# The output projection of a fused attention and gated FFN kernel, in pairs of token tiles with seven products of quarters

## The chip, the cores and the metric

The kernel runs on one core of one Trainium2 chip. The metric is the device time of one launch in microseconds (us); lower is better. A core has five engines that run side by side, each in its own program order, and wait for one another by semaphores: TensorE (PE, matrix products into PSUM; PEld is its weight load), VectorE (DVE), ScalarE (ACT), GpSimd (POOL) and SyncE (SP, which issues DMAs).

## The reference

Four batches, eight heads, 768 tokens, head size 64. Queries and keys are each assigned to the nearest of 16 centroids of their head; a query attends only to keys of its own cluster. The result, as 3072 tokens by 512, goes through a gated FFN:

```python
q_assign = argmax(q_n @ c_n.T); k_assign = argmax(k_n @ c_n.T)      # per head
scores = where(q_assign[:, None] == k_assign[None, :], q @ k.T / sqrt(64), -1e9)
x = softmax(scores) @ v                                             # -> [3072, 512]
gate = 1 / (1 + exp(-(x @ w_gate)))                                 # [512, 1536]
out = (gate * (x @ w_val)) @ w_out                                  # w_out [1536, 512] -> [3072, 512]
```

## The kernel before

**Attention.** The work goes batch by batch and head by head in *steps*. A step multiplies one chunk of 128 keys with half a batch's queries (384): one matmul `sc` of 384 columns (L655), an Exp on ACT into `es` (L660), and, one to three steps later, three matmuls `av` (L678) that add up the values, with a column of ones for the softmax's sum. After a head's last step DVE and POOL normalise (`t`, `rec`, `xp`, L342 to L360), and a transpose puts the result into `xT`. The heads of a later batch are prepared alongside: casts and differences (`hl`, L1217 and L1218), transposes by DMA into `T`, logits against the centroids (`lg`), their sum and maximum on DVE (`lgs` L421, `mx` L432), one-hot rows (`oh` L434, L441), and sums over the values (L302, L308, L309, L318).

**FFN.** `ffn_atoms` makes the work of a block of 384 tokens (half a batch, so eight blocks; t0 is 0 or 384). For each of 12 chunks `fc` of the 1536 hidden columns there is a `gate` (four matmuls of 384 columns, L480, then Tanh on ACT, L488) and a `val` (four matmuls, L500, then DVE's `hT[fc] = (th + 1) * v`, L507, in fp16). Sigmoid is 0.5 (1 + tanh(x/2)); the factor 0.5 is put in when the output leaves PSUM. Then for each of the block's three token tiles `outp` adds up 12 matmuls of 512 columns in one PSUM bank `o` (L520), with `hT` as the stationary operand, `wo` as the moving one; the bank is emptied to `ob` by ACT (L529) or DVE (L527) and stored. The last tile of all is done by `closing` in parts of 256, 128 and 128 columns (`o_end`, L552).

**Order.** Everything is emitted in one order written out by hand; each engine keeps the order in which its instructions are emitted. Attention steps come one after another, preparations at a step named in `SCHED` (`at`, `plan`), and the FFN pieces wait in `queue`. After each step's scores `ffn_run(ns)` takes pieces off the queue for about `ns` nanoseconds of PE time (`ns02`, `ns10` and so on, by batch and quarter), so PE alternates between attention and FFN. The last batch's first block is queued shortly before its attention ends and the last block after it, so most of both runs with no attention beside it.

**PSUM.** Eight banks: a `ring` of four (scores, gates, values, logits), two for `av`, and two (`op`, used in turn) for `o` and, through `turns`, for some transposes and logits.

Of the kernel before, what the change touches and what calls it, by code (L numbers as in the profile page):

```python
# [98 lines left out]
def kernel(  # L99
# [43 lines left out]
    hl2p = pool("hl2", 2)  # L143
    tp = pool("T", 10)
    tbp = pool("TB", 4)
# [9 lines left out]
    osp = pool("os", 3)  # L155
    smp = pool("sm", 3)
# [6 lines left out]

    def turns(n=768, dt=HP, name="turns"):
        return op.tile([128, n], dt, tag="o", name=name)
# [17 lines left out]
    def raw(side):  # L183
        return rawp.tile([128, 2, NCH, 64], FP, tag=f"{side}raw", name=f"{side}raw", bufs=SCHED.get(f"{side}rb", 4))
# [8 lines left out]
    def load(eng, side, b, p):  # L193
        t = RAW[side, b, p] = raw(side)
        eng.dma_start(out=t, in_=view(side, b, p))
# [6 lines left out]
    def load_chunks(eng, side, p, part):  # L202
        if part == 0:
            RAW[side, 0, p] = raw(side)
        c = slice(Q0, NCH) if part else slice(0, Q0)
        eng.dma_start(out=RAW[side, 0, p][:, :, c], in_=view(side, 0, p)[:, :, c])

    def load_half(eng, side, part):
        if (side, 0, 0) not in RAW:
            RAW[side, 0, 0] = raw(side)  # L210
        c = slice(0, Q0) if side == "q" else slice(KC, NCH) if part else slice(0, KC)
        eng.dma_start(out=RAW[side, 0, 0][:, 0, c], in_=view(side, 0, 0)[:, 0, c])
# [36 lines left out]

    c2 = const.tile([128, 2, D], FP, name="c2")  # L250
# [33 lines left out]
    vas = [const.tile([128, 2, NCH, 65], HP, name=f"va{i}") for i in range(6)]  # L284
    for t in vas:
        DVE.memset(t[:, :, :, 64:65], 1.0)
    for t in vss:
        DVE.memset(t[:, :, 64:65], float(NCH))
# [177 lines left out]

    def ffn_atoms(xT, t0, n, b, ch, final=False):
        hT = htp.tile([128, NFC, 384], HP, name="hT")
        gv, outs = [], []
        OA = SCHED.get(f"oa{b}{t0}", SCHED.get("oa", 4))  # L470
        cost = NDC * max(n, 80) / 2.4 + 3

        def gate(fc, st, part):
            def f():
                need(("w", fc // WQ, 0), *(("x", b, p, t0 // 128 + c) for p in range(NP) for c in range(n // 128)))
                if part == 0:
                    st.append(bank(512, name="g"))
                g = st[0]
                for dc in range(GA * part, GA * part + GA):
                    PE.matmul(  # L480
                        out=g[:, 0:n], lhsT=wg[fc // WQ][:, dc, fc % WQ, :],
                        rhs=xT[:, dc, t0 : t0 + n],
                        start=(dc == 0), stop=(dc == NDC - 1),
                    )
                if part < NDC // GA - 1:
                    return
# [6 lines left out]
        def val(fc, st, part):  # L493
            def f():
                need(("w", fc // WQ, 1))
                if part == 0:
                    st.append(bank(512, name="v"))
                w = st[2]
                for dc in range(GA * part, GA * part + GA):
                    PE.matmul(  # L500
                        out=w[:, 0:n], lhsT=wv[fc // WQ][:, dc, fc % WQ, :],
                        rhs=xT[:, dc, t0 : t0 + n],
                        start=(dc == 0), stop=(dc == NDC - 1),
                    )
                if part < NDC // GA - 1:
                    return
                DVE.scalar_tensor_tensor(  # L507
                    hT[:, fc, 0:n], st[1][:, 0:n], 1.0, w[:, 0:n], ALU.add, ALU.mult
                )

            return f

        def outp(t, part, st):
            def f():
                if part == 0:
                    need(*(("wo", i) for i in range(WOP)))
                    st.append(op.tile([128, DM], FP, tag="o", name="o"))
                o = st[0]
                for fc in range(OA * part, OA * part + OA):
                    PE.matmul(  # L520
                        out=o, lhsT=hT[:, fc, bass.ts(t, 128)], rhs=wo[fc // WON][:, fc % WON, :],
                        start=(fc == 0), stop=(fc == NFC - 1),
                    )
                if part == NFC // OA - 1:
                    ob = osp.tile([128, DM], FP, name="ob")
                    if t % 2 or SCHED.get(f"ob{b}{t0}", 0):
                        DVE.tensor_scalar(ob, o, 0.5, None, ALU.mult)  # L527
                    else:
                        ACT.activation(ob, o, AF.Copy, scale=0.5)  # L529

                    def store(ob=ob):
                        SP.dma_start(
                            out=out[b * S : (b + 1) * S].rearrange("(p c) m -> p c m", c=NCH)[
                                :, ch[t], :
                            ],
                            in_=ob,
                        )

                    d_ = SCHED.get("sd", 0)
                    if d_ > 0 and b < B - 2:  # L540
                        at(step_no[0] + d_, store)
                    else:
                        store()

            return f

        def closing(t, a, z):
            def f():
                w = z - a
                o = bank(w, name="o_end")  # L550
                for fc in range(NFC):
                    PE.matmul(  # L552
                        out=o, lhsT=hT[:, fc, bass.ts(t, 128)],
                        rhs=wo[fc // WON][:, fc % WON, a:z],
                        start=(fc == 0), stop=(fc == NFC - 1),
                    )
                ob = osp.tile([128, w], FP, tag="ob_end", name="ob_end")
                if a:
                    DVE.tensor_scalar(ob, o, 0.5, None, ALU.mult)
                else:  # L560
                    ACT.activation(ob, o, AF.Copy, scale=0.5)
                SP.dma_start(
                    out=out[b * S : (b + 1) * S].rearrange("(p c) m -> p c m", c=NCH)[
                        :, ch[t], a:z
                    ],
                    in_=ob,
                )

            return f

        for fc in range(NFC):
            st = []
            for i in range(NDC // GA):
                gv.append((cost * GA / NDC, gate(fc, st, i)))
            for i in range(NDC // GA):
                gv.append((cost * GA / NDC, val(fc, st, i)))
        for t in range(n // 128):
            st = []
            if final and t == n // 128 - 1:
                outs.append([(900, closing(t, a, z)) for a, z in SCHED.get("cl", [(0, 256), (256, 384), (384, 512)])])  # L580
            else:
                outs.append([(OA * 216, outp(t, i, st)) for i in range(NFC // OA)])
        return gv, outs

    queue = []
    GA = SCHED.get("ga", 4)

    def ffn_block(*a):
        gv, outs = ffn_atoms(*a)
        for x in gv:  # L590
            queue.append(x)
        for o in outs:
            queue.extend(o)

    def ffn_two(a, b_):
        gv, outs = ffn_atoms(*a)
        gv2, outs2 = ffn_atoms(*b_)
        seq = gv + gv2[0:2]
        for i, o in enumerate(outs):
            seq += o + gv2[2 + 2 * i : 4 + 2 * i]  # L600
        seq += gv2[2 + 2 * len(outs) :]
        for o in outs2:
            seq += o
        queue.extend(seq)
# [112 lines left out]
    def plan(name, step, f):  # L717
        at(SCHED.get(name, step), f)
# [361 lines left out]
    for x in SCHED.get("lo", ["v0", "k1", "q1", "v1", "k2", "q2", "v2", "k3", "q3", "v3"]):  # L1080
        if x == "v0" and SCHED.get("v0h", 0):
            RAW["v", 0, 0] = raw("v")
# [124 lines left out]
    for i in range(WOP):  # L1207
        plan(f"wo{i}", 44 + 6 * i, lambda i=i: load_wo(i))

# [142 lines left out]
```

## Time and profile before

| | |
|---|---|
| three runs | 326.07, 326.52, 327.12 us, median 326.52 |
| the profiled execution | span 326.4 us from the first to the last instruction; the page gives no other time of it |
| busy shares | PE 97%, weight loads 63%, DVE 57%, ACT 72%, POOL 33% |
| granted TensorE clock | 1.00 in every stretch |
| `o` products | 276 of 512 columns, and 36 narrow ones of the last tile |
| `ob` evacuations | 15 on ACT (596 ns each), 8 on DVE (692 ns each), 3 small ones at the end |
| HBM | 106 GB/s over the span |

How to read the lines: a group's row names the line, engine and operation, out<-in by the program's names, the shape (partitions x elements), the count, then the busy time in us and the mean ns of one, then the engine's idle time just before them and who ended it. A row of a stretch gives the stretch, then the busy us and count of PE, PEld, DVE, ACT, POOL, the granted clock, the DMA share and GB/s. A row of the timeline gives start, length, engine, line, operation, and the idle time before. A PE record is longer than its share of the stream, since matmuls overlap: the pace is read from start to start, as the chain of work does. (The chain gives a product's time from where it takes the array over, so its starts lie up to 0.2 us behind those of the records.)

### The profile page before, as it was taken

The numbers are of one execution on the slowest core, as the hardware profiler recorded it, in microseconds if no ns is written. First come the engines' busy times: TensorE is split into PE (matmuls) and PEld (weight loads), VectorE is DVE, ScalarE is ACT, GpSimd is POOL, SyncE is SP. The second block draws the span as 40 slices with busy tenths as digits, with TensorE's granted clock in tenths as the row PEclk, the third lists the DMA queues.
The fourth block names the chain that finished last, engine by engine and source line by source line (L and its number), as shares of the span: only waits on it lengthen the run. The fifth ranks groups of instructions, "written<-read, shape, count | busy, mean of one in ns | idle before, by whom it ended". The sixth has DMA issues, their size and how long they took to land.

```text
span 326.4 us, 8811 instructions
## 1 busy us (share of the span) xinstructions
PE 318.0 (97%) x3366; PEld 205.8 (63%) x3366; DVE 187.4 (57%) x509; ACT 235.6 (72%) x526; POOL 108.4 (33%) x145
## 2 busy tenths in 40 slices
PE   7899999999999989999999999999999999999996
PEld 4788666766666656666566655666566655654654
DVE  6899567766767766657546655666544322441431
ACT  6788988788899878877677777887778877332420
POOL 6887554054345353324222343323200111000000
PEclk9999999999999999999999999999999999999999
DMA  7999995848977797964795574932731012102002
GB/s 209 358 259 179 263 177 91 207 104 206 242 138 197 138 205 162 257 190 85 124 255 110 169 101 130 238 70 50 141 90 38 2 24 78 44 2 94 6 0 96
DMA packets 77994, 45.14 MB, mean 138 GB/s; under 512 B 56896, under 2 KB 75008, under 8 KB 77952
## 3 DMA queue, kind: packets, MB, share of 16 engines
q1 hardware_dynamic: 73984, 39.73, 50.7%
q0 software_dynamic: 3680, 4.72, 8.7%
q8 instruction: 26, 0.43, 0.5%
q14 instruction: 16, 0.13, 0.1%
q10 hardware_dynamic: 288, 0.13, 0.1%
HBM read 28.34 MB, written 6.29 MB: 106 GB/s over the span
## 4 chain that ended last, share of the span: by engine, by line
PE 86%; DMA 4%; POOL 3%; DVE 3%; issue 2%; SPq 1%; ACT 0%; POOLq 0%
PE g L480 19%; PE v L500 19%; PE o L520 17%; PE sc L655 16%; PE av L678 9%; DMA T<-hl 2%; PE lg L406 2%; DMA kraw<-in_k_dram 2%; PE o_end L552 1%; POOL xp L360 1%; POOL hl L883 1%; POOL hl L1004 1%; PE t_ps L904 0%; PE lg L393 0%; PE t_ps L787 0%
## 5 line engine op out<-in xcount | busy, mean ns | idle before, releaser
L660 ACT ACTIVATE es<-sc 128x384 f16<-128x384 f32 x384 | 175.6, 492 | 42.6 <-PE sc L655 35.6
L655 PE MATMUL sc<-T 128*128 128x384 f16 x384 | 118.0, 325 | 0.7 <-DVE T L985 0.4
L678 PEld LDWEIGHTS <-es 128*128 128x128 f16 x1152 | 81.6, 98 | 49.1 <-ACT es L660 0.2
L678 PE MATMUL av<-va,es 128*128 128x65 f16 x1152 | 97.6, 194 | 0.0
L507 DVE SCALAR_TENSOR_TENSOR hT<-th,v 128x384 f16<-128x384 f32 x96 | 53.1, 554 | 70.3 <-PE av L678 47.4
L500 PE MATMUL v<-xTb,wv 128*128 128x384 f16 x384 | 78.1, 326 | 0.0
L480 PE MATMUL g<-xTb,wg 128*128 128x384 f16 x384 | 78.0, 326 | 0.0
L520 PE MATMUL o<-wo,hT 128*128 128x512 f16 x276 | 75.1, 379 | 0.0
L488 ACT ACTIVATE th<-g 128x384 f32<-128x384 f32 x96 | 47.2, 491 | 25.7 <-DVE hT L507 17.9
L347 POOL TENSOR_TENSOR xp<-t,rec 128x384 f16<-128x384 f32 (+1 forms) x30 | 21.2, 705 | 107.8 <-DVE rec L344 56.4
L480 PEld LDWEIGHTS <-wg 128*128 128x128 f16 x384 | 37.2, 97 | 20.4
L500 PEld LDWEIGHTS <-wv 128*128 128x128 f16 x384 | 37.4, 98 | 19.9
L655 PEld LDWEIGHTS <-T 128*128 128x128 f16 x384 | 37.1, 97 | 1.2 <-DVE T L985 0.7
L520 PEld LDWEIGHTS <-hT 128*128 128x128 f16 x276 | 26.7, 97 | 16.2
L1218 POOL TENSOR_TENSOR hl<-kraw,hl 128x384 f16<-128x384 f32 x22 | 20.4, 925 | 37.5 <-DVE hl L1217 18.2
L342 DVE TENSOR_TENSOR t<-av,sv 128x390 f32<-128x390 f32 (+1 forms) x30 | 14.4, 480 | 20.5 <-PE av L678 16.2
L1218 POOL TENSOR_TENSOR hl<-qraw,hl 128x384 f16<-128x384 f32 x22 | 21.4, 973 | 10.6 <-DVE hl L1217 10.6
L421 DVE TENSOR_REDUCE lgs<-lg 128x192 f32<-128x384 f32 x23 | 12.7, 554 | 13.6 <-PE lg L406 13.6
L529 ACT ACTIVATE ob<-o 128x512 f32<-128x512 f32 x15 | 8.9, 596 | 10.7 <-PE o L520 10.5
L294 POOL CAST va<-vraw 128x768 f16<-128x768 f32 x16 | 13.7, 857 | 2.1 <-DMA vraw<-in_v_dram 2.1
L527 DVE TENSOR_SCALAR ob<-o 128x512 f32<-128x512 f32 x8 | 5.5, 692 | 13.4 <-PE o L520 13.4
L406 PE MATMUL lg<-cm,T 128*128 128x32 f16 x288 | 11.1, 176 | 1.3 <-DMA T<-hl 1.3
(118 smaller groups left out, 239.2 us busy)
## 6 DMA issues: line engine op xcount, KB each, us to landing
vraw<-in_v_dram SPq DMA_DIRECT2D x16, 384.0 KB, 5.9
out_dram<-ob SPq DMA_DIRECT2D x23, 256.0 KB, 2.3
kraw<-in_k_dram SPq DMA_DIRECT2D x15, 384.0 KB, 4.1
qraw<-in_q_dram SPq DMA_DIRECT2D x12, 384.0 KB, 5.0
wg<-in_moe_w_gate_dram POOLq DMA_DIRECT2D x2, 768.0 KB, 9.5
wv<-in_moe_w_val_dram POOLq DMA_DIRECT2D x2, 768.0 KB, 10.5
wo<-in_moe_w_out_dram POOLq DMA_DIRECT2D x2, 768.0 KB, 8.8
qraw<-in_q_dram SPq DMA_DIRECT2D x7, 192.0 KB, 6.9
```

The costliest lines, as they stand in the source:

```text
L342: DVE.tensor_tensor(t[:, 0:nq, :], av, sv, ALU.add)
L347: (eng or POOL).tensor_tensor(x, t[:, 0:nq, 0:64], bcast(rec[:, 0:nq], 64), ALU.mult)
L406: PE.matmul(out=lg[:, bass.ts(i, 32)], lhsT=t[:, c, :], rhs=cm[:, h].rearrange("p s n -> p (s n)"), start=True, stop=True,)
L480: PE.matmul(out=g[:, 0:n], lhsT=wg[fc // WQ][:, dc, fc % WQ, :], rhs=xT[:, dc, t0 : t0 + n], start=(dc == 0), stop=(dc == NDC - 1),)
L488: ACT.activation(th[:, 0:n], g[:, 0:n], AF.Tanh, scale=0.5)
L500: PE.matmul(out=w[:, 0:n], lhsT=wv[fc // WQ][:, dc, fc % WQ, :], rhs=xT[:, dc, t0 : t0 + n], start=(dc == 0), stop=(dc == NDC - 1),)
L507: DVE.scalar_tensor_tensor(hT[:, fc, 0:n], st[1][:, 0:n], 1.0, w[:, 0:n], ALU.add, ALU.mult)
L520: PE.matmul(out=o, lhsT=hT[:, fc, bass.ts(t, 128)], rhs=wo[fc // WON][:, fc % WON, :], start=(fc == 0), stop=(fc == NFC - 1),)
L655: PE.matmul(out=sc.rearrange("p (c t) -> p c t", t=128), lhsT=s["k"], rhs=s["q"], start=True, stop=True,)
L660: ACT.activation(es, sc, AF.Exp, scale=SCALE)
L678: PE.matmul(out=av[:, a0 + s["c0"] + i, :], lhsT=s["es"][:, bass.ts(i, 128)], rhs=VA[b, p][:, e, s["j"], :], start=(first and i == 0 and a ...
L1218: POOL.tensor_tensor(hl[:, :, 64:128], r, hl[:, :, 0:64], ALU.subtract)
```

## The change

Tokens are taken in pairs of tiles A1 (t1) and A2 (t2), hidden columns in halves f = 0, 1 (six chunks each), output columns in halves of 256. B11, B12, B21, B22 are the quarters of `w_out`. In place of eight products of quarters there are seven (Strassen's scheme in Winograd's form):

- once, four mixed weights (`mix_wo`, each in two parts of 128x768, while the gates of the first block run): T1 = B12 - B11 and T2 = B22 - T1 on DVE, T3 = B22 - B12 and T4 = B21 - T2 on POOL. They lie in `held`, the raw tiles of the first batch's last head pair, which are of no more use then, and T4 in B12's place.
- per pair, four sums on DVE in fp16 (`pair_sums`, 128x768 each): s1 = A2[0] + A2[1], s2 = s1 - A1[0], s4 = A1[1] - s2, s3 = A1[0] - A2[0]. The first two come right after the block's last `hT`, or, for the second pair of a block, after the first pair's p15; the other two after P1.
- per pair, seven products of six matmuls of 256 columns (`pair_out`), by turns in two banks x and y, each continued or restarted as listed, with what reads the bank afterwards:

| product | bank | operands | then |
|---|---|---|---|
| P1 | x, new | A1[0] B11 | ACT copies p1 |
| P4 | y, new | A2[1] T4 | DVE p14 = y + p1 |
| P2 | x, added to P1 | A1[1] B21 | ACT copies to ob of t1, left half |
| P6 | y, added to P4 | s2 T2 | DVE p16 = y + p1 |
| P5 | x, new | s1 T1 | DVE p15 = x + p1 |
| P7 | y, added to P6 | s3 T3 | DVE ob of t2 = y + p14, and y + p15 |
| P3 | x, added to P5 | s4 B22 | DVE ob of t1, right half = x + p16 |

Where the table says "new" the bank is overwritten, else the product adds to what lies there.

Pairs are (0, 1) for the first block of a batch and (2, 3), (4, 5) for the second, so there are twelve, and the first block's third tile is done with the second block. The next pair's P1 takes the bank that the last P3 did not use. While a pair is under way, `turns` takes its bank from the ring. The factor 0.5 moves: the ones column becomes 2, which halves x, so Tanh needs no scale and the output no factor. To make room, `T` has 8 buffers for 10, `va` 5 for 6, raw inputs 3 for 4. The `ns` of the quarters are some 3.5% smaller (all but `ns10`), and `lag01` is 8 for 4.5.

```diff
-    tp = pool("T", 10)
-    tbp = pool("TB", 4)
+    tp = pool("T", 8)
...
+    def mix_wo(i, c, eng):
+        done.add(("wt", i, c))
+        o, a, z, f = [
+            (T1, B12, B11, ALU.subtract), (T3, B22, B12, ALU.subtract),
+            (T2, B22, T1, ALU.subtract), (T4, B21, T2, ALU.subtract),
+        ][i]
+        c = slice(3 * c, 3 * c + 3)
+        eng.tensor_tensor(o[:, c], a[:, c], z[:, c], f)
...
-                ACT.activation(th[:, 0:n], g[:, 0:n], AF.Tanh, scale=0.5)
+                ACT.activation(th[:, 0:n], g[:, 0:n], AF.Tanh)
...
+                if fc == NFC - 1:
+                    sums[0]["one"]()
...
+        def one():
+            add(1, tok(b, t2, 0), tok(b, t2, 1), ALU.add)
+            add(2, st[1], tok(b, t1, 0), ALU.subtract)
+
+        def two():
+            add(4, tok(b, t1, 1), st[2], ALU.subtract)
+            add(3, tok(b, t1, 0), tok(b, t2, 0), ALU.subtract)
...
+        def end1():
+            copy(acc("p1"), st["x"])
+            sm["two"]()
+
+        def end4():
+            plus(acc("p14"), st["y"], st["p1"])
...
+        def end5():
+            plus(acc("p15"), st["x"], st["p1"])
+            if after:
+                after()
+
+        def end7():
+            plus(st["ob", 1][:, lo_], st["y"], st["p14"])
+            plus(st["ob", 1][:, hi_], st["y"], st["p15"])
+            store(1, t2)
+
+        def end3():
+            plus(st["ob", 0][:, hi_], st["x"], st["p16"])
...
+        steps = [
+            ("x", A(t1, 0), B11, True, end1), ("y", A(t2, 1), T4, True, end4),
+            ("x", A(t1, 1), B21, False, end2f), ("y", M(2), T2, True, end6),
+            ("x", M(1), T1, True, end5), ("y", M(3), T3, False, end7),
+            ("x", M(4), B22, False, end3),
+        ]
...
+                for c in range(g, g + G):
+                    PE.matmul(
+                        out=st[z], lhsT=a[:, c, :], rhs=rhs[:, c, :],
+                        start=start and c == 0, stop=c == HF - 1, skip_group_check=True,
+                    )
```

More of the change, by code (lines that the diff above doesn't have):

```diff
@@ L155 @@
     osp = pool("os", 3)
+    accp = pool("acc", 1)
     smp = pool("sm", 3)
@@ L504, in f @@
                     )
-                if part < NDC // GA - 1:
-                    return
                 DVE.scalar_tensor_tensor(
-                    hT[:, fc, 0:n], st[1][:, 0:n], 1.0, w[:, 0:n], ALU.add, ALU.mult
+                    HB[b, blk][:, fc, 0:n], st[0][:, 0:n], 1.0, w[:, 0:n], ALU.add, ALU.mult
                 )
[L511 to L567, printed above, removed]
+                if fc == NFC - 1:
+                    sums[0]["one"]()
@@ L583, in ffn_atoms, with tok @@
-        return gv, outs
+            gv.append((cost, gate(fc, st)))
+            gv.append((cost, val(fc, st)))
+        pairs = [(0, 1)] if blk == 0 else [(2, 3), (4, 5)]
+        sums = [pair_sums(b, *x) for x in pairs]
+        outs = []
+        for i, x in enumerate(pairs):
+            after = sums[i + 1]["one"] if i + 1 < len(pairs) else None
+            outs += pair_out(b, *x, sums[i], after, final and i + 1 == len(pairs))
+        return gv, outs
+    def tok(b, t, f):
+        return HB[b, t // 3][:, HF * f : HF * f + HF, bass.ts(t % 3, 128)]
@@ new lines, in pair_sums, with add @@
+    def pair_sums(b, t1, t2):
+        st = {}
+        engs = {"D": DVE, "P": POOL}
+        who = SCHED.get("sumE", "DDDD")
+        def add(i, a, z, f):
+            t = hl2p.tile([128, 2, 3, 128], HP, tag="hl2", name=f"s{i}")
+            st[i] = t.rearrange("p a c t -> p (a c) t")
+            engs[who[i - 1]].tensor_tensor(st[i], a, z, f)
+        def one():
[4 more added lines that the diff above has]
+            add(3, tok(b, t1, 0), tok(b, t2, 0), ALU.subtract)
+        st.update(one=one, two=two)
+        return st
```

148 lines of the change are left out of this document (99 added, 49 removed), and 8 rows, old and new, of the table SCHED.

## The prediction

> **What bounds the kernel now.** I read the page first: its busy shares and its chain of work. Then the same chain in order of time and a table of stretches, to see whether the busy TensorE is full or only looks so, and last the groups of instructions kept apart by shape.
>
> ```profile
> span 326.4 us, 8811 instructions
> PE 318.0 (97%) x3366; PEld 205.8 (63%) x3366; DVE 187.4 (57%) x509; ACT 235.6 (72%) x526; POOL 108.4 (33%) x145
> PE 86%; DMA 4%; POOL 3%; DVE 3%; issue 2%; SPq 1%; ACT 0%; POOLq 0%
> ```
>
> PE carries 86% of the chain. The chain in order of time shows how closely its products follow one another (start, length, what):
>
> ```profile
> 154.20 0.09 PE av L678 x3
> 154.29 0.16 PE sc L655
> 154.45 0.43 PE o L520 x2
> 154.88 0.09 PE av L678 x3
> ...
> 157.03 0.29 PE lg L406 x12
> ...
> 290.76 0.65 PE g L480 x4
> ...
> 292.06 7.77 PE o L520 x36
> ...
> 320.61 2.66 PE o_end L552 x36
> ```
>
> One step of attention at 154 us is three av (0.09), one sc (0.16) and two o (0.43): 0.68 us, and the next step starts 0.68 us later. Nothing is idle in between. So a column that is no longer streamed is time saved, and a wait of PE is time lost, at the full price.
>
> ```profile
> 130.00:154.00 24.00, 24.00 (x241) 15.67 (x239) 14.41 (x39) 19.12 (x44) 8.76 (x11) 1.00 0.72 176
> 154.00:166.00 12.00, 12.00 (x123) 6.94 (x122) 6.36 (x16) 7.93 (x18) 3.22 (x4) 1.00 0.83 179
> ```
>
> Columns: stretch, PE, PEld, DVE, ACT, POOL busy, granted clock. In a gate/value stretch (first row) and in an output stretch (second) PE is full at clock 1.00, and VectorE has 40 to 47% free.
>
> **Term 1: the streamed columns.** An o product of 512 columns costs 7.77/36 = 0.216 us, a g of 384 costs 0.65/4 = 0.1625: 0.42 ns a column and 2.5 ns, so 256 columns cost 0.109 and 128 cost 0.056. The 36 narrow products of o_end (12 of 256, 24 of 128) then make 2.65; the chain has 2.66.
>
> ```profile
> L520 PE MATMUL o<-wo,hT 128*128 128x512 f16 x276 | 75.1, 379 | 0.0
> L520 PEld LDWEIGHTS <-hT 128*128 128x128 f16 x276 | 26.7, 97 | 16.2
> ```
>
> Now: 276 x 0.2158 + 2.66 = 62.2 us. After: 12 pairs x 7 products x 6 = 504 of 256 columns, 55.0 us. **-7.2 us.** The 216 added weight loads (97 ns each) cost nothing, because o_end already loads for every 256 or 128 columns and keeps the pace of its columns.
>
> **Term 2: who PE waits for.** The seven products go by turns into two PSUM banks: P1 x, P4 y, P2 x, P6 y, P5 x, P7 y, P3 x. P6 adds onto P4 in bank y, so it must not start before VectorE has read P4 (p14 = y + p1). In VectorE's instruction order of the changed program there stand, between the block's last hT and p14, all four sums of halves (s1, s2, s4, s3, 128x768 fp16) and whatever attention work falls there. VectorE takes them in order. These are its prices:
>
> ```profile
> L507 DVE SCALAR_TENSOR_TENSOR hT<-th,v 128x384 f16<-128x384 f32 x96 | 53.1, 554 | 70.3 <-PE av L678 47.4 <-PE v L500 22.6
> L421 DVE TENSOR_REDUCE lgs<-lg 128x192 f32<-128x384 f32 x23 | 12.7, 554 | 13.6 <-PE lg L406 13.6
> L342 DVE TENSOR_TENSOR t<-av,sv 128x390 f32<-128x390 f32 x18 | 10.1, 561 | 6.2 <-PE av L678 5.6 <-POOL hl L1218 0.6
> L434 DVE TENSOR_TENSOR oh<-lgs,mx 128x96 f16<-128x96 f32 x42 | 9.4, 266 | 0.7
> L1217 DVE CAST hl<-qraw 128x384 f16<-128x384 f32 x22 | 10.3, 467 | 0.0
> L1217 DVE CAST hl<-kraw 128x384 f16<-128x384 f32 x22 | 7.9, 359 | 0.0
> L302 DVE TENSOR_TENSOR va<-vraw 128x384 f32<-128x384 f32 x12 | 7.6, 636 | 0.0
> L432 DVE TENSOR_REDUCE mx<-lgs 128x12 f32<-128x192 f32 x21 | 7.4, 353 | 0.7
> L309 DVE TENSOR_TENSOR vs<-va,va 128x128 f16<-128x128 f32 x12 | 5.1, 425 | 0.4
> L308 DVE TENSOR_TENSOR va<-va 128x128 f32<-128x128 f32 x12 | 4.3, 359 | 0.1
> L342 DVE TENSOR_TENSOR t<-av,sv 128x195 f32<-128x195 f32 x12 | 4.3, 359 | 14.3 <-PE av L678 10.6 <-issue 2.0 <-POOL hl L1218 1.7
> L441 DVE TENSOR_SCALAR oh<-oh 128x96 f16<-128x96 f16 x22 | 4.2, 189 | 0.8
> L344 DVE RECIPROCAL rec<-t 128x6 f32<-128x6 f32 x18 | 3.5, 192 | 0.6
> L318 DVE TENSOR_SCALAR sv<-vs_ps 128x130 f32<-128x130 f32 x12 | 3.5, 290 | 0.6 <-PE vs_ps L313 0.6
> L917 DVE COPY T<-t_ps 128x768 f16<-128x768 f16 x6 | 3.3, 550 | 0.0
> ```
>
> No row has a sum of two fp16 tensors of 768. From below it is bounded by the 16-bit copy of 768, 0.55 us; from above by the two-input sum of 32-bit data, where 195 elements take 0.359 and 390 take 0.561, so 1.04 ns an element and 0.95 at 768. I take 0.55, since type and width are those of the copy. The Trainium skill, VectorE: DVE Perf Modes (The perf-mode tier table), puts a tensor_tensor of 16-bit data in SBUF at two results a cycle, 1224 ns for 2048; worked out from that it would be an estimated 0.56 us, and the sum below would be the same to 0.5 us. No run here shows it yet. The evacuations of 256 columns (p14, p16, p15 and three ob) are two-input sums with a PSUM source, 0.42 by the two t rows.
>
> ```profile
> 154.09 0.93 DVE L302 TENSOR_TENSOR va<-vraw 128x384 f32<-128x384 f32 x1
> 155.05 0.29 DVE L308 TENSOR_TENSOR va<-va 128x128 f32<-128x128 f32 x1
> 291.89 7.93 PE L520 MATMUL o<-wo,hT 128*128 128x512 f16 x36
> 292.16 0.55 DVE L507 SCALAR_TENSOR_TENSOR hT<-th,v 128x384 f16<-128x384 f32 x1 [0.75 <-PE v L500]
> ```
>
> Between two instructions VectorE loses 0.03 us, and the last hT ends 0.82 us after the first output product starts.
>
> In the closing stretches, where no attention is left: s1 starts at 0.85, p14 ends at 0.85 + 4 x 0.58 + 0.45 = 3.62, and PE hears of it some 0.06 later. PE has P1, P4 and P2 done after 18 x 0.109 = 1.97. It waits 1.7 us. During the attention steps PE has more to do in between (av and sc, 0.25 a step, and lg), but VectorE too. Fourth pair: s1, s2, L308, L309, s4, s3, L421, L432, twice L434, L441, p14 make 5.03 and 12 gaps, 5.39 us, against 3.27 on PE; wait 0.91 + 5.39 - 3.27 = 3.0. The same count for each pair that opens a block's projection (VectorE from s1 to p14; PE from P1 to P6; wait):
>
> pair 1: 5.22, 3.91, 2.2; pair 2: 4.47, 4.02, 1.4; pair 4: 5.39, 3.27, 3.0; pair 5: 3.90, 3.03, 1.8; pair 7: 4.28, 3.52, 1.7; pair 8: 3.09, 3.22, 0.8; pairs 10 and 11: 2.77, 1.97, 1.7 each. Sum 14.3. (The VectorE evacuations of now, eight of 512 columns, are gone from these counts, which go by the changed order.)
>
> The second pair of a block waits elsewhere. Its s1 and s2 stand on VectorE ahead of the two ob that empty bank y after P7, and its P1 needs that bank. In the last block: P5 ends, p15 is done 0.71 later, s1, s2 and both ob take 2.06, so the bank is free after 2.83, while PE has only P7 and P3 (1.31): wait 1.5, and 0.1 more at P6. Pairs 3, 6, 9 and 12 so come to 2.7, 3.0, 0.8 and 1.6, sum 8.1. **+22.4 us** (with 0.95 a sum: +40).
>
> What is queued behind a waiting P6 or P1 on PE is the next sc and av, so ACT runs dry and catches nothing up: PE had no idle time for it.
>
> **Term 3: the end.**
>
> ```profile
> 315.26 5.34 PE L520 MATMUL o<-wo,hT 128*128 128x512 f16 x24
> 323.30 0.29 DVE L559 TENSOR_SCALAR ob_end<-o_end 128x128 f32<-128x128 f32 x1 [0.38 <-PE o_end L552]
> ```
>
> Now the last evacuation ends 0.5 us behind PE (315.26 + 5.18 + 2.66 = 323.10). After the change three ob of 0.45 stand in a row there and end about 0.96 behind, and the last store is twice as large as the last of now: **+0.7** (0 to 1.5). Two pairs in place of three tiles in the last block move columns from the attention to the end, which is no cost where PE is full in both.
>
> **Term 4: the mixed weights.** Eight differences of 128x768, four on VectorE (2.3 us) and four on GpSimd, fall among the gates of the first block, between hT evacuations for which the ring's banks wait. Instructions are only added there, so it is no gain: from 0 to 2.3; GpSimd is a third busy and its part is off the path. I take **+0.8**.
>
> At nothing: the halved softmax and tanh scale (same instructions), 24 ScalarE copies of 256 for 15 of 512 (ACT is 72% busy, and the copy of p1 has P4 as cover; its delay falls inside the wait for p14), fewer buffers for T, va and raw inputs. In the third batch one load of v now stands on SP ahead of the cast that frees its buffer, for about two steps, 1.5 us; the transposes behind it are due tens of steps later. If that cover is gone, it costs those 1.5 once.
>
> **Sum:** 326.4 - 7.2 + 22.4 + 0.7 + 0.8 = 343.1. The profiled execution's span (326.4) is 0.1 under the median of the runs (326.52), and the page gives no other time of it. I say 343.
>
> **Rivals.**
> *Half the waits.* The attention work among the sums costs less than its rows say, because part of it is early or late by a step. With it gone altogether from in front of the sums and evacuations, the opening pairs wait 5.1 in all and the second ones 3.1, so 329; with half of it left, 336; I put this case at 333. For it: a mean hides spread (the row of L302 says 0.636, the one above took 0.93). Against: the order is fixed, and in-order work is not skipped. 0.14.
> *One element a cycle.* The sums take 0.95: 361. For it: all two-input rows with 32-bit data do. Against: the 16-bit rows. 0.12.
> *Faster: the steps cover it.* If inside the attention no pair waits, and only pairs 10 to 12 pay 5.1: 326.4 - 7.2 + 5.1 + 0.7 = 325.0. It decides at P6: VectorE would have to be through with four sums, the attention rows and p14 within PE's 3.0 to 4.0 us less 0.9. With 0.2 us a sum the count above still leaves 7.6, so both the sums and the rows would have to shrink. For it: VectorE has 40% free. 0.05.
> *The loads set the pace.* If a weight load did not hide behind 256 columns, 216 more of 97 ns: +21, 364. Against: the o_end row, 56 ns for 128 columns with a load each. 0.01. The Trainium skill, TensorE: Matmul & The Clock Gate (Back-to-back issue gap), gives about 81 ns for 128 columns and 131 for 512 in a stream of loads and matmuls; by that pace 288 products would cost 38 us now and 504 of 256 an estimated 49, so the change would lose 11 where I let it gain 7.2. The trace disagrees at both ends: 56 and 216.
>
> **Chances.** Forecast 0.68, with its own range of 337 to 351 (a sum at 0.5 to 0.65, the bounds of terms 3 and 4); the others as above. Less than 1 us (0.3%) is about what a measurement of this kernel can't tell from no change: faster 0.04, same 0.02, slower 0.94. The range takes in the half-waits case and goes part of the way to the one-element case, which with the covered case is left out: 331 to 356.
>
> **What would show it.** Right: output products 0.109 us apart in the profile after, PE idle of 1 to 3 us ahead of P6 with the VectorE p14 sum as releaser, at the end 1.7 us each; the sums at 0.55. Wrong: sums far from 0.55, PE full in the output stretches, or PE's longest waits on something else, such as DMA or ScalarE's copies.

## The result, and the profile after

The changed kernel takes 345.86 us (median of four runs, 344.54 to 346.24) against 326.73 (four runs, 326.07 to 327.12): ratio 1.058, 95% interval 1.055 to 1.060. It is 19 us slower. The forecast was 343.0, range 331 to 356. The profiled execution of after is its lowest run (344.54, span 342.8, mean granted clock 0.998); its other three have a mean clock of 0.99 and spans of 343.8 to 344.4. Where a run lists both, its time is some 1.8 us more than its span.

The page after, its busy shares and its chain of work:

```profile
span 342.8 us, 9334 instructions
PE 316.8 (92%) x3558; PEld 228.0 (67%) x3558; DVE 238.7 (70%) x622; ACT 235.1 (69%) x534; POOL 116.7 (34%) x149
PE 75%; DVE 17%; issue 3%; POOL 3%; DMA 1%; DVEq 0%; POOLq 0%
```

VectorE has gained 51 us of work, and its part of the chain has gone from 3% to 17%. The stretches tell where TensorE is no longer full (columns as in the prediction):

```profile
52.00:66.00 14.00, 10.34 (x126) 6.99 (x122) 12.64 (x22) 7.83 (x20) 11.22 (x9) 1.00 0.63 152
...
130.00:154.00 24.00, 23.15 (x256) 16.30 (x255) 16.84 (x52) 18.72 (x43) 8.91 (x12) 1.00 0.73 173
154.00:166.00 12.00, 11.79 (x134) 8.14 (x133) 8.23 (x21) 9.03 (x21) 4.84 (x5) 1.00 0.59 153
```

Two places show: single waits of half a microsecond to two at the output products (the second row lacks 0.85 us, most of it one such wait; both later rows were full before), and one bad stretch, 52 to 66 us, where the weights are mixed (the first row lacks 3.66). The groups of instructions by shape name the first (qheld and kheld hold T2 and T1, so these products are P6 and P5):

```profile
L671 PE MATMUL o<-wo,hT 128*128 128x256 f16 x216 | 31.4, 272 | 3.7 <-DVE ob L614 2.9 <-DVE sv L345 0.8
L671 PE MATMUL o<-qheld,s 128*128 128x256 f16 x72 | 11.1, 272 | 9.2 <-DVE p L614 9.2
L671 PE MATMUL o<-kheld,s 128*128 128x256 f16 x72 | 11.0, 272 | 0.0
L561 DVE TENSOR_TENSOR s<-hT 128x768 f16<-128x768 f16 x24 | 15.6, 649 | 0.3
L561 DVE TENSOR_TENSOR s<-s,hT 128x768 f16<-128x768 f16 x12 | 7.3, 607 | 0.4
L561 DVE TENSOR_TENSOR s<-hT,s 128x768 f16<-128x768 f16 x12 | 6.6, 548 | 0.1
L614 DVE TENSOR_TENSOR p<-o,p 128x256 f32<-128x256 f32 x36 | 15.1, 419 | 10.2 <-PE o L671 9.5 <-ACT p L611 0.4
```

P6 waits 9.2 us by the records, always for a VectorE evacuation `p`; P5 waits for nothing. The rest, 3.7 us in the first row, stands ahead of P1 and P4. One such wait in the timeline, in the last block (start, length, engine, line; idle before; the row of 18 products is P1, P4 and P2):

```profile
326.90 2.13 PE L671 MATMUL o<-wo,hT 128*128 128x256 f16 x18
327.17 0.55 DVE L529 SCALAR_TENSOR_TENSOR hT<-th,v 128x384 f16<-128x384 f32 x1 [0.75 <-PE v L524]
...
327.76 0.56 DVE L561 TENSOR_TENSOR s<-hT 128x768 f16<-128x768 f16 x1
328.35 0.56 DVE L561 TENSOR_TENSOR s<-s,hT 128x768 f16<-128x768 f16 x1
328.94 0.56 DVE L561 TENSOR_TENSOR s<-hT,s 128x768 f16<-128x768 f16 x1
...
329.42 0.55 DVE L561 TENSOR_TENSOR s<-hT 128x768 f16<-128x768 f16 x1
329.89 0.42 DVE L614 TENSOR_TENSOR p<-o,p 128x256 f32<-128x256 f32 x1
330.36 0.82 PE L671 MATMUL o<-qheld,s 128*128 128x256 f16 x6 [1.33 <-DVE p L614]
331.01 0.82 PE L671 MATMUL o<-kheld,s 128*128 128x256 f16 x6
```

Four sums, then p14, which ends at 330.31, and PE goes on at 330.36: the picture that the prediction drew. (The table of the change, and the prediction after it, say that P6 adds to P4 in bank y. In the code P6 starts the bank afresh; the wait for p14's read of the bank is the same either way.)

The balance is counted from the starts of all PE records of a trace. By the streaming price of the prediction (0.42 ns a column and 2.5 ns) the streamed work falls from 308.1 to 300.8 us. The narrow products of 16 and 32 columns follow each other at 25 ns in both traces, which adds the same 5.6 to each. TensorE's idle time beyond that rises from 6.4 us (in the profile of an ordinary execution of before, below) to 31.0. Of these 24.5 us, 15.1 stand ahead of output products, 5.0 between 38 and 66 us, 2.1 between 81 and 112 us, and 2.3 in small pieces elsewhere. From the start of the last product to the end it takes 4.12 us where it took 3.40. Sum: -7.3 + 24.5 + 0.7 = +17.9, and the spans differ by 18.0 (342.8 against 324.8). The medians differ by 19.1; the rest goes with the lower clock of three of the four executions (last section).

### The profile page after: what moved, and what is told of

Its sections match the earlier page's. It is cut to its first block, busy times and chain, and to the rows that moved or that the text cites. A ratio compares the mean times of both kernels' runs of the same rounds, so it can differ in the third digit from the quotient of the medians.

```text
span 342.8 us, 9334 instructions
## 1 busy us (share of the span) xinstructions
PE 316.8 (92%) x3558; PEld 228.0 (67%) x3558; DVE 238.7 (70%) x622; ACT 235.1 (69%) x534; POOL 116.7 (34%) x149
## 4 chain that ended last, share of the span: by engine, by line
PE 75%; DVE 17%; issue 3%; POOL 3%; DMA 1%; DVEq 0%; POOLq 0%
PE g L508 18%; PE v L524 17%; PE sc L739 15%; PE o L671 11%; PE av L762 8%; DVE s L561 5%; DVE hT L529 2%; PE lg L433 1%; DVE ob L614 1%; PE lg L420 1%; DVE p L614 1%; PE t_ps L988 1%; PE oh_ps L1048 1%; DMA T<-hl 1%; DVE lgs L448 1%
## 5 line engine op out<-in xcount | busy, mean ns | idle before, releaser
L374 POOL TENSOR_TENSOR xp<-t,rec 128x384 f16<-128x384 f32 (+1 forms) x30 | 22.2, 740 | 107.2 <-DVE rec L371 61.2
L671 PEld LDWEIGHTS <-s 128*128 128x128 f16 x288 | 27.9, 97 | 16.3 <-issue 10.5
L671 PE MATMUL o<-wo,hT 128*128 128x256 f16 x216 | 31.4, 272 | 3.7 <-DVE ob L614 2.9
L671 PEld LDWEIGHTS <-hT 128*128 128x128 f16 x216 | 21.0, 97 | 9.9 <-issue 5.5
L1305 POOL TENSOR_TENSOR hl<-qraw,hl 128x384 f16<-128x384 f32 x22 | 20.7, 941 | 13.7 <-DVE hl L1304 13.7
L614 DVE TENSOR_TENSOR p<-o,p 128x256 f32<-128x256 f32 x36 | 15.1, 419 | 10.2 <-PE o L671 9.5
L671 PE MATMUL o<-qheld,s 128*128 128x256 f16 x72 | 11.1, 272 | 9.2 <-DVE p L614 9.2
L561 DVE TENSOR_TENSOR s<-hT 128x768 f16<-128x768 f16 x24 | 15.6, 649 | 0.3
L614 DVE TENSOR_TENSOR ob<-o,p 128x256 f32<-128x256 f32 x36 | 13.5, 416 | 2.2 <-PE o L671 2.0
```

The costliest lines, as they stand in the source:

```text
L374: (eng or POOL).tensor_tensor(x, t[:, 0:nq, 0:64], bcast(rec[:, 0:nq], 64), ALU.mult)
L561: engs[who[i - 1]].tensor_tensor(st[i], a, z, f)
L614: DVE.tensor_tensor(dst, a, z, ALU.add)
L671: PE.matmul(out=st[z], lhsT=a[:, c, :], rhs=rhs[:, c, :], start=start and c == 0, stop=c == HF - 1, skip_group_check=True,)
L1305: POOL.tensor_tensor(hl[:, :, 64:128], r, hl[:, :, 0:64], ALU.subtract)
```

## The experiments

The theory was that VectorE's queue sets the waits: sums that nothing needs yet stand ahead of an evacuation that PE waits for. The rivals were that the evacuations alone, the mixed weights, the weight loads or the smaller buffers cost the time.

**The sums later.** Only the order on VectorE is changed: s4 and s3 behind p14, and the next pair's s1 and s2 behind the evacuations of P7. All instructions stay.

```diff
         def end1():
             copy(acc("p1"), st["x"])
-            sm["two"]()
         def end4():
             plus(acc("p14"), st["y"], st["p1"])
+            sm["two"]()
         def end5():
             plus(acc("p15"), st["x"], st["p1"])
-            if after:
-                after()
         def end7():
             ...
+            if after:
+                after()
```

> The changed kernel with two sums moved in VectorE's order: s4 and s3 stand behind p14 instead of ahead of it, and the next pair's s1 and s2 behind the two ob of P7 instead of ahead of them. Same instructions, same data. Theory (VectorE's queue): the waits in front of P6 (10.6 us of idle TensorE in the changed kernel's trace) fall by up to 1.2 each, in the closing stretch from 1.50 to about 0.3, and the waits in front of the second pairs' P1 (3.6 us) to about 1; a part comes back in front of P7, where p16 now stands behind s4 and s3 (about 0.3 each). Time 336 to 339 us. Rival (the hand-over of a bank costs this much by itself, whatever stands in the queue): the waits stay at 1.5 and the time at 345 to 347.

Measured 338.10 us (337.94 to 338.37), ratio 1.036 (1.034 to 1.038), 7.8 less than the median of after. Some of that is the clock of after's other executions: between the two profiled ones, both at a mean clock of 0.998, the spans differ by 6.6 (342.8 and 336.2). The same place in its timeline of VectorE and PE (start, length, engine, line; idle before):

```profile
322.20 0.56 DVE L561 TENSOR_TENSOR s<-hT 128x768 f16<-128x768 f16 x1
322.79 0.56 DVE L561 TENSOR_TENSOR s<-s,hT 128x768 f16<-128x768 f16 x1
323.26 0.42 DVE L614 TENSOR_TENSOR p<-o,p 128x256 f32<-128x256 f32 x1
...
321.34 2.13 PE L671 MATMUL o<-wo,hT 128*128 128x256 f16 x18
323.74 0.82 PE L671 MATMUL o<-qheld,s 128*128 128x256 f16 x6 [0.27 <-DVE p L614]
```

P6 follows P1 by 2.40 us where it took 3.46, and the wait shrinks from 1.33 to 0.27. Nothing but the order was changed, so this share of the waits is shown to be order: at all products together 15.1 us become 8.8. What stays is mostly 3.0 ahead of P6, 1.9 ahead of P7, for p16 behind the moved sums (more than expected), and 3.5 ahead of P4, up to 1.77 at once, most of it for `ob` evacuations.

**No sums.** The products take halves of hT in place of the sums (the sums are left out of the computation); everything else stays.

```diff
-            add(1, tok(b, t2, 0), tok(b, t2, 1), ALU.add)
-            add(2, st[1], tok(b, t1, 0), ALU.subtract)
+            st[1], st[2] = tok(b, t2, 0), tok(b, t2, 1)
...
-            add(4, tok(b, t1, 1), st[2], ALU.subtract)
-            add(3, tok(b, t1, 0), tok(b, t2, 0), ALU.subtract)
+            st[4], st[3] = tok(b, t1, 1), tok(b, t1, 0)
```

> The changed kernel without the 48 sums per token pair set: P6, P5, P7 and P3 take halves of hT themselves, so the output is another. All products, evacuations, mixed weights and stores stay. Theory: idle TensorE in front of the products falls from 15.3 us to under 2, the rest of the added idle time (about 7 us, mixed weights and VectorE lagging in the steps) falls to about 5; time 328 to 331 us, still slower than before the change. Rival (hand-over): about 1.5 us per pair stays in the closing stretch and the time is over 338.

Measured 332.01 us (331.56 to 332.24): 13.9 less than after (13.0 between the profiled spans), and a little above the range expected. TensorE's idle time at the products falls from 15.1 to 2.4 us. From 38 to 66 us its products still come 4.9 us late, of which some 1.5 are a stretch at half clock (last section). The sums are the larger part of the loss, not all of it.

**The mixed weights all on VectorE.** `"DPDP"` becomes `"DDDD"` in the plan of `mix_wo`: GpSimd's four differences go to VectorE.

> The changed kernel with all eight differences of weights on VectorE, none on GpSimd. Theory: the 5 us of idle TensorE around 55 to 68 us come from the GpSimd differences (1.6 to 1.9 us each), ahead of which other work of GpSimd waits and beside which two-input VectorE instructions take 1.3 to 2.0 us in place of 0.27 to 0.55; without them the idle time there falls to 1 to 2.5 and the time by 2.5 to 4, to 342 to 343.5 us. Rival (VectorE is simply full there): four more differences of 0.55 make it worse, 347 to 348.

Measured 343.04 us (342.28 to 343.88), 2.8 less than after (2.3 between the profiled spans), with four more instructions on the engine that the kernel waits for. The timelines of PE, VectorE and GpSimd in after show two reasons:

```profile
59.58 0.51 PE L871 MATMUL t_ps<-identh,hl 128*128 128x128 f16 x6 [1.96 <-POOL hl L851]
...
64.89 0.81 PE L524 MATMUL v<-xTb,wv 128*128 128x384 f16 x4 [1.57 <-DVE hT L529]
...
57.33 1.41 DVE L1125 TENSOR_TENSOR oh<-lgs,mx 128x96 f16<-128x96 f32 x1
...
60.60 0.93 DVE L275 TENSOR_TENSOR qheld<-wo,kheld 128x768 f16<-128x768 f16 x1
...
61.92 1.99 DVE L851 TENSOR_TENSOR hl<-kraw,hl 128x384 f16<-128x384 f32 x1
...
65.14 1.14 DVE L902 TENSOR_TENSOR oh<-lgs,mx 128x96 f16<-128x96 f32 x1
...
56.69 1.94 POOL L275 TENSOR_TENSOR vheld<-wo,wo 128x768 f16<-128x768 f16 x1
58.59 0.92 POOL L851 TENSOR_TENSOR hl<-qraw,hl 128x384 f16<-128x384 f32 x1
59.48 1.64 POOL L275 TENSOR_TENSOR vheld<-wo,wo 128x768 f16<-128x768 f16 x1
...
61.85 1.63 POOL L275 TENSOR_TENSOR wo<-wo,qheld 128x768 f16<-128x768 f16 x1
64.52 1.64 POOL L275 TENSOR_TENSOR wo<-wo,qheld 128x768 f16<-128x768 f16 x1 [1.03 <-DVE qheld L275]
```

The first wait, 1.96 us, is for an instruction of the attention (`hl`) that stands in GpSimd's own queue behind a difference and starts at 58.59, as that ends. The other is for `hT`, which stands in VectorE's queue behind an `hl` that took 1.99 us. For such lengths the rows give a reason. Each of GpSimd's differences (ends 58.63, 61.12, 63.48, 66.16) has a VectorE instruction under it that ends only just after: at 58.74, 61.53, 63.91 and 66.28. All four read two tensors in SBUF, and they end 0.1 us (96 elements) or 0.4 us (384 and 768) after GpSimd. Spans on GpSimd are rough, but four out of four say that VectorE stood still until GpSimd was through. The sums of halves bear it out: all six that take over 0.7 us in after end 0.4 us behind a two-input GpSimd instruction. The Trainium skill, SBUF — State Buffer (Who interferes with whom), says that a VectorE instruction with two SBUF inputs contends with a GpSimd instruction that reads SBUF, for a port pair that only one of them holds at a time; these rows agree. With GpSimd's differences gone, the timeline of this experiment has the same instruction at a fourth of its length:

```profile
61.43 0.55 DVE L851 TENSOR_TENSOR hl<-kraw,hl 128x384 f16<-128x384 f32 x1
```

TensorE's idle time from 38 to 66 us goes from 5.3 to 3.1, not to the 1 to 2.5 expected. The edit takes away both reasons at once, so their shares are not told apart.

**The other half of the bank.** P6, P5, P7 and P3 write columns 256 to 511 of the bank that the earlier products used, so that they need not wait for its reader.

```diff
+            st["x2"], st["y2"] = u[x][:, HD:DM], u[1 - x][:, HD:DM]
...
-            ("x", A(t1, 1), B21, False, end2f), ("y", M(2), T2, True, end6),
+            ("x", A(t1, 1), B21, False, end2f), ("y2", M(2), T2, True, end6),
```

> The changed kernel with the products by turns in four halves of the two banks, which so far used one half each: P6 and P7 go into y's other half, P5 and P3 into x's other half, so P6 and P5 wait for no reader. VectorE's order is unchanged. Theory: no wait is left in front of P6; p14 and p16 now have to be done before P7, which in the closing stretch leaves about 0.9 in place of 1.5 a pair, and nearly nothing in the steps, where more work of TensorE stands in between; the second pairs' P1 still waits. Time 336 to 340 us. Rival (VectorE's total work in the output stretches is the bound, the place of the wait does not matter): 344 to 346.

Measured 345.66 us (344.50 to 346.44), as after, and not the 336 to 340 expected. Its list of waits:

```profile
PE o L672 <- DVE p L615: 9.2, 8, 1.7
```

P6 waits as before, and for the same instruction: the program's wait goes by the bank, not by its columns. The Trainium skill, PSUM — Partial Sum Buffer (PSUM bank collisions raise a hardware error), asks for such a guard, by bank in its simple form and not by address; no run here shows what happens without it. The experiment doesn't tell the theories apart.

**Four banks in the last batch.** The same edit with true banks: for the last three pairs the second products go into two banks of the ring.

```diff
+            st["x2"], st["y2"] = (bank(HD), bank(HD)) if b == B - 1 else (st["x"], st["y"])
```

> The changed kernel; in the last batch's three pairs alone P6 and P7 use a PSUM bank of their own from the ring, and P5 and P3 another, so that P6 and P5 share no bank with what VectorE still has to read (e4_half_banks used the other half of the same bank, and its waits stayed at 1.50 us with the p14 sum as releaser). Theory: no wait in front of P6; in pairs 10 and 11 a wait of 0.6 to 0.9 in front of P7, which needs p16, in place of 1.50; no wait of the 12th pair's P1 (1.07). Time 343 to 344.8 us. Rival (VectorE is the bound of these pairs wherever the wait stands): the waits only move, 345 to 346.5.

Measured 341.85 us (341.12 to 343.38), 4.0 less than after by the medians and better than expected. Its timeline of PE in the last block:

```profile
327.87 2.13 PE L672 MATMUL o<-wo,hT 128*128 128x256 f16 x18
329.94 0.83 PE L672 MATMUL bank<-qheld,s 128*128 128x256 f16 x6
...
331.66 0.82 PE L672 MATMUL bank<-vheld,s 128*128 128x256 f16 x6 [0.24 <-DVE p L615]
...
332.97 2.15 PE L672 MATMUL o<-wo,hT 128*128 128x256 f16 x18
```

P6 now follows P2 without idle time though all four sums still stand ahead of p14: the wait was for the bank, not for the sums' data. P7 waits 0.24, and the next pair's P1 not at all. By the count of starts the waits of pairs 10 to 12 fall from 1.50 + 1.49 + 1.07 in after to twice 0.40 ahead of P7 and twice 0.10 ahead of P6, so by 3.1. The two executions near full clock (341.12 and 341.29) lie 3.3 under the one of after (344.54); the rest of the 4.0 is the mix of clocks in the medians.

**Products only.** Neither sums nor mixed weights (T1 to T4 are quarters of `w_out` as they are); the seven products and all evacuations stay.

```diff
-    T1, T2, T3, T4 = half(held["k"]), half(held["q"]), half(held["v"]), B12
+    T1, T2, T3, T4 = B12, B22, B21, B12
```

> The changed kernel without the sums of halves and without the eight differences of weights: the seven products take halves of hT and quarters of the weights as they are, so the output is another. Products, their order, evacuations, stores and buffers stay. Theory: what is left of e2_no_sums over the kernel before (332.0 against 326.4 us) is the weights' differences: about 4.5 us of idle TensorE around 52 to 70 us and a lower granted clock behind it, so the time falls by 4.5 to 6.5 more, to 325.5 to 327.5. Rival (the evacuations, six a pair on VectorE, are as dear): it stays at 329 to 332.

Measured 326.35 us (325.83 to 326.87) against 326.78 for before in the same runs, ratio 0.998 (0.997 to 0.999). From 38 to 66 us TensorE idles 0.5 us, so that stretch is the mixed weights' doing. But 7.3 us of columns are saved and 0.4 us come out. Idle time of 6.5 us has come in after 38 us: 2.0 at products, the rest in pieces up to 1.0 us at scores and logits, and the end is longer. Some pieces stand in after as they do here (0.53 ahead of `x_ps` and 0.89 ahead of `sc`, at 83 and 85 us there, 76 and 78 here), so neither sums nor mixed weights make them. Which of the moved instructions does was not tried, nor were the changed step budgets (`ns`, `lag01`) alone.

**Before, profiled again**, unchanged, as an ordinary execution of it was wanted.

> The kernel before, unchanged, for a second profile. The first profile of it has a span of 326.4 us, the other executions of it some 324.6. Theory: the first profiled execution held a single late transposing DMA (1.5 us of idle TensorE at 122 us, in front of lg), so here the span is 324.4 to 324.9 and that idle piece is gone. Rival: a profiled execution is always longer, span 326 to 327 with the same piece.

Measured 326.60 us with a span of 324.8. The first profile of before had a span of 326.4: in it TensorE waited 1.5 us at 122 us for a DMA, and here it does not.

**The smaller buffers alone** in the kernel before (`T` 8 for 10, `va` 5 for 6, raw inputs 3 for 4).

> The kernel before with the changed kernel's smaller pools alone: 8 buffers for T in place of 10, 5 for va in place of 6, 3 for each raw input in place of 4 with the first batch's last pair in tiles of its own. Theory (priced at nothing in the prediction): 326.0 to 327.0 us. Rival: loads or transposes wait for a free buffer and hold the SP queue, 328 to 330.

Measured 326.54 us (326.25 to 327.04), ratio 0.999 (0.998 to 1.000): they cost nothing.

**Quarter columns alone** in the kernel before: each o product of 512 columns is done as two of 256 with a weight load each, eight products of quarters in place of seven.

```diff
+                    for z in range(2):
                         PE.matmul(
-                            out=o, lhsT=hT[:, fc, bass.ts(t, 128)],
+                            out=o[:, bass.ts(z, 256)], lhsT=hT[:, fc, bass.ts(t, 128)],
```

> The kernel before with each of the 276 output products of 512 columns made as two of 256 columns, with a weight load each: same sums, same evacuations. Theory (the columns set the pace, 0.109 us for 256): 552 x 0.109 against 276 x 0.216 is +0.7 us, so 326.8 to 327.5. Rival (a weight load of 97 ns does not hide behind 256 columns): +27, about 353; or in part, over 330.

Measured 327.81 us (326.79 to 328.22), ratio 1.002 (1.001 to 1.003), so 1.0 more than before and a little above the range expected; the added products, at 2.5 ns each, say 276 x 2.5 ns = 0.7. Its PE group of the line:

```profile
L521 PE MATMUL o<-wo,hT 128*128 128x256 f16 x552 | 75.8, 272 | 0.0
```

276 more weight loads, and no idle time in front of any product: they hide.

**Sums later and mixing on VectorE together.**

> The changed kernel with both edits that helped: the sums behind the evacuations as in e1_sums_late, and all differences of weights on VectorE as in e3_mix_on_vector. Theory (two separate causes in two stretches): the gains add, 345.9 - 7.8 - 2.8 = 335.3; range 334.5 to 336.5, still slower than before. Rival (one cause, VectorE's and GpSimd's joint load): less than the sum, 337 to 338.

Measured 336.34 us (335.66 to 337.37), ratio 1.029 (1.027 to 1.032). Sums later gave 7.8; with them in place, the mixing gives 1.8 more. Between profiled spans at a clock of 0.998 or 0.999 it is 6.6 and 2.3 alone and 8.6 together. The two causes are almost separate, and the kernel is still slower than before.

**Quiet pairs.** If waits make the loss, the scheme should pay where VectorE is least used. Seven products for only two of the twelve pairs (the third batch's second block, beside the attention of the last batch), sums late, mixing on VectorE, one difference every four steps ahead of them; the other tiles as in the kernel before, with step budgets to suit.

```diff
-        pairs = [(0, 1)] if blk == 0 else [(2, 3), (4, 5)]
+        pairs = [(2, 3), (4, 5)] if (b, blk) == QUIET else []
```

> Seven products only for two pairs (four token tiles, the third batch's tile 2 and its second block), which run beside the last batch's attention, where VectorE is busy 24 to 42 percent; all other tiles have twelve products of 512 columns and the evacuations of before. Sums behind the evacuations, the differences of weights on VectorE, one every four steps, ahead of them, in tiles of their own; the small sum over v of the last two head pairs in the ring, and step budgets that follow the moved tile. Theory (a gain of 0.6 us of columns a pair, and waits only where VectorE is full): 2 x 0.6 less 0 to 0.5 of waits, 325.5 to 326.3 beside 326.4 to 326.8 for the kernel before, so faster by 0.2 to 0.4 percent. Rival (the scheme's evacuations cost as much as it saves anywhere): 326.6 to 327.5.

Measured 326.44 us (twelve runs, 325.73 to 327.54) against 326.75 (seventeen runs), ratio 0.9991 (0.9978 to 1.0003): not to be told from no change, and a little above the 325.5 to 326.3 expected. Its page:

```profile
span 325.1 us, 8927 instructions
PE 317.9 (98%) x3402; PEld 210.3 (65%) x3402; DVE 198.4 (61%) x535; ACT 234.2 (72%) x527; POOL 109.7 (34%) x145
```

TensorE is full again, with 0.1 us of idle time ahead of the pairs' products, so the waits can be avoided; what is left of the gain, 1.2 us by the columns of two pairs, is too small to show.

In a row, by medians, with the difference to the line above:

| kernel | us | |
|---|---|---|
| before | 326.7 | |
| products and evacuations alone | 326.35 | -0.4 |
| with mixed weights, no sums | 332.0 | +5.7 |
| with all (after) | 345.9 | +13.9 |
| sums later | 338.1 | -7.8 |
| and mixing on VectorE | 336.3 | -1.8 |

## Why the prediction was right

The forecast was 2.9 us under the median and on the right side, by the mechanism that it named. Two of its terms missed by several microseconds each, in opposite directions, and 4.4 us of idle time stood in no term, so that the sum came this close is in part luck.

**Columns, right.** -7.2 was said and -7.3 counted; products stand 0.108 us apart (P6 at 330.36 and P5, six later, at 331.01 in the timeline above). The rival that the loads set the pace is refuted by the quarter columns, which cost 1.0 us for 276 loads. By the pace that the Trainium skill, TensorE: Matmul & The Clock Gate (Back-to-back issue gap), gives for loads and products in turn they would cost an estimated 18 us (276 of 131 ns become 552 of some 98); the run disagrees.

**Waits for VectorE's queue, right in kind, too large.** 22.4 was said, 15.1 counted: 10.6 of 14.3 at the pairs that open a projection, 4.5 of 8.1 at the second pairs of a block. Place and releaser are mostly as said: 10.6 of all stand ahead of P6 for p14 and 2.9 ahead of a second pair's P1 for the two ob. The other 1.6 stand ahead of P4, where none was forecast: 0.9 in the eighth pair, for `sv` of the attention, and 0.7 in the sixth, for `ob`. In the closing stretch 1.50 came of 1.7. The step that failed most is "between two instructions VectorE loses 0.03 us". It was read from a pair in which the second instruction uses the first one's result. The fourth pair, in VectorE's timeline of after:

```profile
165.23 0.56 DVE L561 TENSOR_TENSOR s<-s,hT 128x768 f16<-128x768 f16 x1
165.70 0.28 DVE L335 TENSOR_TENSOR va<-va 128x128 f32<-128x128 f32 x1
...
166.23 0.55 DVE L561 TENSOR_TENSOR s<-hT,s 128x768 f16<-128x768 f16 x1
166.70 0.55 DVE L561 TENSOR_TENSOR s<-hT 128x768 f16<-128x768 f16 x1
167.17 0.55 DVE L448 TENSOR_REDUCE lgs<-lg 128x192 f32<-128x384 f32 x1
167.75 0.35 DVE L459 TENSOR_REDUCE mx<-lgs 128x12 f32<-128x192 f32 x1
...
168.70 0.42 DVE L614 TENSOR_TENSOR p<-o,p 128x256 f32<-128x256 f32 x1
```

Where an instruction needs the one before (lgs, mx, oh), it starts 0.03 us after its end. Where it doesn't (166.23 to 166.70 to 167.17), it starts 0.08 before that end. From s1 (164.63) to the end of p14 (169.12) it took 4.49 us for the 5.39 counted (0.7 less by the spacing, 0.2 by shorter `va` and `vs` rows), s1 stood 0.60 behind P1 instead of 0.85, and PE, which needed the 3.27 said, waited 1.87 for the 3.0 said. Over the seven opening pairs in which P6 waits, 13.5 was counted and 9.65 came: the spacing makes -3.6, the earlier s1 -1.3, more work on PE in the first pair -0.8, and three sums of some 1.2 us +1.9. The length of the sums was right: 0.55 taken, 0.55 to 0.56 in the timeline above. The estimate of 0.56 by the Trainium skill, VectorE: DVE Perf Modes (The perf-mode tier table), agrees with that. The means of the sums, 0.607 and 0.649, hold single ones of up to 1.18 us, such as the one at 200.62, which ends 0.41 us behind a multiplication on GpSimd.

**The end, right.** +0.7 was said and 0.72 counted.

**Mixed weights, too small.** 0.8 was said, with bounds of 0 and 2.3. With the weights' stretch 5.0 us of idle time came, and the ladder has 5.7 for them. The step that failed is "GpSimd is a third busy and its part is off the path". A share of busy time says nothing about whom GpSimd holds up: its four differences of 1.6 to 1.9 us kept VectorE waiting and GpSimd's own next instruction too, and the rows of before had a hint of the first (0.93 us for an L302 whose mean is 0.636).

**At nothing.** Buffers and weight loads: shown to be so. But the products-only kernel shows about 4.5 us of idle time away from the products that the prediction had nowhere, and after has 4.4 outside the products and the weights' stretch. What makes it stays open.

**Base.** The profiled execution that the sum began from was 1.6 us longer than an ordinary one, and 1.8 us lie outside a span. The two nearly cancel (326.4 and 326.7), so by luck the base did no harm; the profiled rise was 18.0 us where the terms said 16.7.

**Rivals.** Half the waits (333): the waits came to two thirds, but not for its reason: the attention's rows kept their length within 0.2 us in the sum over those seven pairs. One element a cycle: refuted by 0.55 us. Covered (325.0): not so here; with neither sums nor mixed weights it comes close, and even then only 0.4 us are gained.

## What to carry to other kernels

A product saved on a full engine is worth its columns only if no other engine's queue gets longer ahead of something that the full engine waits for: read the order on the helping engine between the last instruction that PE needed and the next one that it will need. If work must be added there, put it behind the evacuation, or give the next product another bank, before trying to make the work itself shorter. An addition on GpSimd is not free for being on an idle engine, when VectorE works on two SBUF tensors beside it or when the full engine waits for what stands behind it in GpSimd's queue.

## What the hardware showed beyond that

VectorE and GpSimd shut each other out, with the numbers above: a 0.55 us difference took 1.99. And TensorE's clock can halve in mid-kernel. In the kernel without sums two stretches (columns as before), inside a wait for GpSimd and after it, show it:

```profile
59.00:59.40 0.40, 0.00 (x0) 0.00 (x0) 0.40 (x2) 0.00 (x0) 0.40 (x2) 1.00 0.70 111
...
60.00:62.00 2.00, 2.00 (x24) 1.41 (x23) 1.76 (x4) 0.81 (x2) 2.00 (x3) 0.50 1.09 356
```

and its timeline of PE:

```profile
59.41 0.79 PE L869 MATMUL t_ps<-identh,hl 128*128 128x128 f16 x6 [1.95 <-POOL hl L849]
...
61.44 1.49 PE L524 MATMUL v<-xTb,wv 128*128 128x384 f16 x4
```

After a wait of 1.95 us the granted clock is 0.50 for 3.4 us (59.47 to 62.88), and four products of 384 columns take 1.49 us, where the four at 63.06 take 0.81, so some 1.5 us are lost. The Trainium skill, TensorE: Matmul & The Clock Gate (What's actually happening), puts the return to half clock after an idle window of about 3.4 us; here 1.95 us did it. The length of the wait alone does not decide it: in the profiled execution of after a wait of 1.96 us at the same place left the clock at 1.00, while that of four banks, at a mean clock of 0.989, has two spells of 3.4 us at 0.50, from 61.08 and from 78.15, the second behind a wait of only 1.22 us (for p14 in the first pair). After's other executions, at a mean clock of 0.99, took 1.1 to 1.7 us longer; two such spells would fit, but no trace of those was taken.
